# Forty-eight columns of weights, not eight, in the small products of an attention and feed-forward kernel

## The chip, the cores and the metric

The kernel runs on one core of a Trainium2 chip. The metric is the device time of one execution in microseconds (us). Before the change three runs took 989.1, 990.55 and 991.38 us, a median of 990.55 us. Beside these runs one execution was profiled; it took 990.49 us, of which 988.7 us lie between its first and its last instruction (its span).

## The reference

Linear attention with a decaying state, over 4 sequences, 8 heads, 768 steps and 48 elements per head, followed by two feed-forward layers over the 3072 tokens.

```python
for t in range(S):
    cur = np.einsum('bhd,bhe->bhde', u[None] * kt, vt)
    y[:, :, t] = np.einsum('bhd,bhde->bhe', rt, state + cur)
    state = w[None, :, :, None] * state + np.einsum('bhd,bhe->bhde', kt, vt)
x = y as (3072 tokens, 384)
x = (sigmoid(x @ w_gate) * (x @ w_val)) @ w_out      # d_ff 1536
x = (relu(x @ w_in) ** 2) @ w_out2                   # d_ff 2048
```

## The kernel before

**Attention.** The 768 steps are cut into 6 chunks of 128, and a unit is one chunk of one sequence: 24 units. Heads lie in pairs, one on partitions 0 to 47 and one on 64 to 111, and a chunk is two halves of 64 steps. So the attention's products are small: 48 or 64 rows of contraction, 48 or 64 columns of weights, 48 or 64 moving columns, in float32. Each product is two passes, and each pass is a weight load (PEld) and a matrix product (PE) in the trace. Depending on the partitions that a product reads and writes, it runs in one of four quarters of the array (called a tile of the array below): rows 0 to 63 or 64 to 127, output partitions 0 to 63 or 64 to 127. All these products write into one buffer of three PSUM banks, `att`.

For unit n `attn_out` (line 331) issues on TensorE, in this order: 16 products with `am` as moving operand (L270, `att<-am,kv`), 8 that read the state (`reads(0)`, L270), a call of `settle`, the 16 score products of unit n+1 (`attn_scores`, `att<-rT,kT`), a call of `settle` (at the head of `attn_sums`), the 16 sums of unit n+1 (`att<-kv`), a call of `settle`, and 8 more reads (`reads(1)`). After that ScalarE copies the results from PSUM and the sync queue sends them off. `settle` (line 275) is one product of the first 48 partitions of an operand of this unit; its output `tok` is a buffer of the tag `v`, the same one that `pv` of the feed-forward layers uses, and nothing reads it. Over the kernel `settle` is called 72 times: once in `attn_sums(0)`, three times in each of 23 units and twice, without anything between, in the last, which has no unit after it.

**Feed-forward.** Each weight matrix is split into a high and a low float32r part (`convert`: DVE, ScalarE and GpSimd work on each piece), and each product is then three products of 128x128 weights with 512 moving columns (L429 and L448). The order of all instructions is written out by hand: phases 0 to 4 of the first layer run over chunks 0 to 4 with the attention units of the next chunk between their products. `fill(f, j)` calls the attention steps at fixed slots; `attn_out` comes between the gate product (`pg`) and the value product (`pv`). From phase 5 on there are feed-forward products alone.

The first four units run before the first feed-forward phase, with dummy products (`warm`, L590) between them. Units 4 to 7 lie in phase 0, while weights are still loaded and converted; units 8 to 23 in phases 1 to 4.

Of the kernel before, what the change touches and what calls it, by code (L numbers as in the profile page):

```python
# [19 lines left out]
B, H, S, D = 4, 8, 768, 48  # L20
# [22 lines left out]
def tile_kernel(  # L43
# [12 lines left out]
    nc = tc.nc  # L56
# [218 lines left out]
    def settle(x):  # L275

        tok = pp.tile([P, T], F32, tag="v", name="tok")
        nc.tensor.matmul(tok[0:8, 0:8], lhsT=x[0:D, 0:8], rhs=x[0:D, 0:8], start=True, stop=True)  # L278

    def attn_scores(n):  # L280

# [13 lines left out]
    def attn_sums(n):  # L295

        if n >= NU:
            return
        kv = kv_t[n]
        settle(kv)  # L300
        for j in range(HP):
            for q in range(2):
                h = 2 * j + q
                for a in range(2):
                    x = slice(a * L, (a + 1) * L)
                    mm64(
                        1 - a,
                        q,
                        pu[a][64 * q : 64 * q + width[q], j],
                        kv[x, HD + h * D :][:, : width[q]],  # L310
                        kv[x, h * D :][:, :D],
                    )
# [18 lines left out]
    def attn_out(n):  # L331
# [18 lines left out]
        for j in range(HP):  # L350
            for q in range(2):
                h = head(q, j)
                for a in range(2):
                    x = slice(a * L, (a + 1) * L)
                    mm(a, q, j, width[q], kv[x, h * D :][:, : width[q]], am[x, h])
        reads(0)
        settle(kv)
        attn_scores(n + 1)
        attn_sums(n + 1)
        settle(kv)  # L360
        reads(1)
        while len(kv_t) <= n + (4 if len(kv_t) < IN_W + 2 else 3) and len(kv_t) < NU:
# [386 lines left out]
```

## Time and profile before

| what | value |
|---|---|
| median of 3 runs | 990.55 us |
| profiled execution | 990.49 us, span 988.7 us |
| PE busy | 961.3 us (97%), 6904 instructions |
| PEld busy | 764.3 us (77%) |
| DVE, ACT, POOL busy | 453.1, 401.8, 135.0 us |
| mean granted TensorE clock | 0.976 |

PE is TensorE at its products, PEld the same engine at its weight loads, DVE VectorE, ACT ScalarE, POOL GpSimd. The start of a product in the trace is what can be compared; its end is modelled. A product that is the first of a group has its record begin together with its weight load, so its 0.25 to 0.27 us hold the load too, and in a stream one lasts 0.21 or 0.22 us.

### The profile page before, as it was taken

The page shows a single profiled execution, that of the slowest core. Times are in us where ns is not written, and L with a number is a line of the kernel's source. Part 1 is how long each engine was busy: PE and PEld are TensorE (multiplying, and loading weights), DVE is VectorE, ACT ScalarE, POOL GpSimd, SP SyncE. Part 2 cuts the span into 40 slices and gives each one's busy share as a digit, 9 for nine tenths or more (in the row PEclk, how much of TensorE's full clock was granted, in tenths as well). Part 3 has the DMA queues.
Part 4 walks back from the last instruction along what each step waited for, and adds up shares of the span by engine and source line. Part 5 has one row for each costly group of instructions (what it writes and reads, how often), then busy time and mean ns, then how long its engine had stood idle before and what let it go on. Part 6 is the DMA issues. An engine that isn't in the chain of part 4 may idle for free.

```text
span 988.7 us, 16639 instructions
## 1 busy us (share of the span) xinstructions
PE 961.3 (97%) x6904; PEld 764.3 (77%) x6904; DVE 453.1 (46%) x742; ACT 401.8 (41%) x826; POOL 135.0 (14%) x121
## 2 busy tenths in 40 slices
PE   6888899999999999999999999999999999999997
PEld 3566688888888888887888888888888888888886
DVE  5667757754434444422344465343333433433332
ACT  3656756533233223322366564232332322323322
POOL 6446735300000000000033121000000000000000
PEclk7679899999999999999999999999999999999999
DMA  8664555522122221100244440010100100100000
GB/s 302 203 211 126 169 167 161 147 79 84 52 60 89 90 67 27 68 7 15 95 128 123 154 155 1 1 64 1 33 32 1 64 1 1 65 1 1 32 0 33
DMA packets 42235, 76.86 MB, mean 78 GB/s; under 512 B 5168, under 2 KB 17584, under 8 KB 42160
## 3 DMA queue, kind: packets, MB, share of 16 engines
q1 hardware_dynamic: 42160, 75.80, 24.1%
q8 instruction: 54, 0.88, 0.4%
q14 instruction: 21, 0.17, 0.1%
HBM read 60.05 MB, written 11.01 MB: 72 GB/s over the span
## 4 chain that ended last, share of the span: by engine, by line
PE 90%; DVE 4%; ACT 2%; issue 1%; POOL 1%; DMA 1%; SPq 0%; DVEq 0%; ACTq 0%
PE pg L429 34%; PE two L448 16%; PE pv L429 14%; PE po L448 11%; PE att L448 7%; PE att L270 5%; PE pw L590 1%; PE tok L278 1%; DVE first L239 1%; DMA first<-in_rkv 1%; DVE am L319 1%; ACT am L255 1%; POOL wu L134 0%; DVE raw L156 0%; DVE mid L388 0%
## 5 line engine op out<-in xcount | busy, mean ns | idle before, releaser
L429 PE MATMUL pg<-xh,wu 128*128 128x512 f32 x1008 | 315.0, 397 | 5.8 <-ACT wu L133 3.7
L429 PEld LDWEIGHTS pg<-xh,wu 128*128 128x128 f32 x1008 | 189.8, 188 | 54.2 <-ACT wu L133 5.0
L429 PE MATMUL pg<-xl,wu 128*128 128x512 f32 x504 | 195.0, 395 | 0.0
L576 ACT CAST gh<-s 128x512 fp32r<-128x512 f32 (+1 forms) x169 | 104.9, 621 | 194.0 <-DVE s L572 120.6
L412 DVE TENSOR_TENSOR gl<-s,gh 128x512 fp32r<-128x512 f32 x162 | 113.3, 699 | 86.6 <-PE po L448 56.3
L575 DVE TENSOR_TENSOR s<-s 128x512 f32<-128x512 f32 (+1 forms) x97 | 66.6, 687 | 181.4 <-ACT s L574 181.4
L448 PE MATMUL two<-gh,wu 128*128 128x512 f32 x472 | 148.1, 395 | 0.0
L429 PE MATMUL pv<-xh,wu 128*128 128x512 f32 x432 | 141.2, 408 | 0.4 <-POOL wu L134 0.4
L574 ACT ACTIVATE s<-pg 128x512 f32<-128x512 f32 (+1 forms) x97 | 57.6, 594 | 190.3 <-PE pg L429 190.3
L572 DVE TENSOR_TENSOR s<-pv,s 128x512 f32<-128x512 f32 x72 | 49.6, 689 | 176.1 <-PE pv L429 172.6
L429 PEld LDWEIGHTS pg<-xl,wu 128*128 128x128 f32 x504 | 95.0, 189 | 22.7 <-DVE xl L412 0.3
L448 PEld LDWEIGHTS two<-gh,wu 128*128 128x128 f32 x472 | 89.3, 189 | 21.7
L448 PE MATMUL po<-gh,wu 128*128 128x512 f32 (+1 forms) x338 | 105.5, 392 | 0.0
L429 PEld LDWEIGHTS pv<-xh,wu 128*128 128x128 f32 x432 | 81.1, 191 | 21.0 <-POOL wu L134 0.8
L448 PE MATMUL two<-gl,wu 128*128 128x512 f32 x236 | 92.5, 392 | 0.0
L558 ACT ACTIVATE s<-pg 128x512 f32<-128x512 f32 x72 | 43.6, 606 | 110.5 <-PE pg L429 110.2
L429 PE MATMUL pv<-xl,wu 128*128 128x512 f32 x216 | 86.8, 402 | 0.0
L448 PEld LDWEIGHTS po<-gh,wu 128*128 128x128 f32 x338 | 63.4, 188 | 14.6
L154 ACT ACTIVATE raw<-raw 128x384 bf16<-128x384 bf16 x68 | 73.6, 1082 | 0.0
L448 PE MATMUL po<-gl,wu 128*128 128x512 f32 (+1 forms) x169 | 66.2, 392 | 0.0
L448 PE MATMUL att<-gh,wu 128*128 128x512 f32 (+1 forms) x204 | 63.4, 392 | 0.0
L255 ACT ACTIVATE am<-anti,dv 128x64 f32<-128x64 f32 x192 | 50.1, 340 | 16.5 <-DVE dv L245 16.5
(295 smaller groups left out, 919.6 us busy)
## 6 DMA issues: line engine op xcount, KB each, us to landing
raw<-in_w SPq DMA_DIRECT2D x68, 384.0 KB, 3.2
kv<-in_rkv SPq DMA_DIRECT2D x16, 384.0 KB, 3.3
xin<-x2d SPq DMA_DIRECT2D x6, 768.0 KB, 4.2
out<-x2s SPq DMA_DIRECT2D x18, 256.0 KB, 2.0
first<-in_rkv SPq DMA_DIRECT2D x16, 256.0 KB, 5.8
kT<-in_rkv SPq DMA_DIRECT2D x16, 256.0 KB, 4.5
rT<-in_rkv SPq DMA_DIRECT2D x16, 256.0 KB, 5.0
x2d<-x2s SPq DMA_DIRECT2D x15, 256.0 KB, 2.0
```

The costliest lines, as they stand in the source:

```text
L154: nc.scalar.activation(top, top, AF.Prelu, scale=2.0**-112, alpha=2.0**32)
L239: nc.vector.tensor_mul(t, t, two)
L255: nc.scalar.mul(am_t[n][:, h], anti, dv_t[n][:, h : h + 1])
L270: nc.tensor.matmul(out, lhsT=lhsT, rhs=rhs, start=(bank, q) not in opened, stop=True, skip_group_check=True)
L412: (eng or nc.vector).tensor_tensor(out=dst, in0=src, in1=high.bitcast(F32), op=ALU.subtract)
L429: nc.tensor.matmul(ps, lhsT=a, rhs=b_, start=(i == 0), stop=(i == len(pairs) - 1))
L448: nc.tensor.matmul(po[k][:, ts], lhsT=a, rhs=b_[:, ts], start=(first and m == 0), stop=(last and m == 2 and ts is cuts[-1]),)
L558: nc.scalar.activation(s, pg, AF.Sigmoid)
L572: nc.vector.tensor_tensor(out=s[:, ts], in0=pv[:, ts], in1=s[:, ts], op=ALU.mult)
L574: nc.scalar.activation(s[:, ts], pg[:, ts], AF.Relu)
L575: nc.vector.tensor_mul(s[:, ts], s[:, ts], s[:, ts])
L576: nc.scalar.copy(gh[:, ts], s[:, ts])
```

## The change

The product in `settle` takes 48 columns of weights and writes 48 partitions, where it took and wrote 8. Rows, moving columns, buffer and the places of the calls stay.

```diff
     def settle(x):
         tok = pp.tile([P, T], F32, tag="v", name="tok")
-        nc.tensor.matmul(tok[0:8, 0:8], lhsT=x[0:D, 0:8], rhs=x[0:D, 0:8], start=True, stop=True)
+        nc.tensor.matmul(tok[0:D, 0:8], lhsT=x[0:D, 0:D], rhs=x[0:D, 0:8], start=True, stop=True)
```

## Rows read from the trace of the kernel before

**Rows 1.** The page: span, PE's busy time, chain that ended last.
```profile
span 988.7 us, 16639 instructions
...
PE 961.3 (97%) x6904; PEld 764.3 (77%) x6904; DVE 453.1 (46%) x742; ACT 401.8 (41%) x826; POOL 135.0 (14%) x121
...
PE 90%; DVE 4%; ACT 2%; issue 1%; POOL 1%; DMA 1%; SPq 0%; DVEq 0%; ACTq 0%
```

**Rows 2.** Stretches: length, then busy us and count by engine; clock, DMA.
```profile
0.00:127.00 127.00, 104.66 (x1342) 73.66 (x1346) 86.40 (x132) 71.28 (x183) 70.87 (x67) 0.81 0.62 199
127.00:450.00 323.00, 322.94 (x3266) 259.41 (x3266) 156.95 (x278) 124.43 (x305) 29.65 (x22) 1.00 0.27 83
450.00:988.70 538.70, 533.65 (x2316) 431.26 (x2306) 209.70 (x332) 206.09 (x339) 34.50 (x32) 1.00 0.14 46
```

**Rows 3.** Waits of the weight loads, 127 to 450 us: total, times, longest.
```profile
PEld att L270 <- issue: 5.8, 16, 0.4
PEld tok L278 <- PE tok L278: 0.2, 1, 0.2
```

**Rows 4.** Timeline of one unit on TensorE: start, us, engine, line, operation.
```profile
404.46 0.39 PE L429 MATMUL pg<-xl,wu 128*128 128x512 f32 x1
404.78 0.54 PEld L270 LDWEIGHTS att<-am,kv 64*64 64x64 f32 x32 [0.36 <-issue]
404.78 0.68 PE L270 MATMUL att<-am,kv 64*64 64x64 f32 x32
405.22 0.12 PEld L270 LDWEIGHTS att<-rT,state 48*48 48x48 f32 x1
...
405.34 0.21 PE L270 MATMUL att<-rT,state 48*48 48x64 f32 x1
...
405.45 0.21 PE L270 MATMUL att<-rT,state 48*48 48x64 f32 x1
...
405.47 0.21 PE L270 MATMUL att<-rT,mid 48*48 48x64 f32 x1
405.61 0.10 PEld L278 LDWEIGHTS tok<-kv 48*8 48x8 f32 x2
405.62 0.20 PE L278 MATMUL tok<-kv 48*8 48x8 f32 x2
405.74 0.56 PEld L270 LDWEIGHTS att<-rT,kT 48*64 48x64 f32 x32
405.74 0.69 PE L270 MATMUL att<-rT,kT 48*64 48x64 f32 x32
406.37 0.09 PEld L278 LDWEIGHTS tok<-kv 48*8 48x8 f32 x2
406.50 0.54 PEld L270 LDWEIGHTS att<-kv 64*64 64x64 f32 x32
407.09 0.10 PEld L278 LDWEIGHTS tok<-kv 48*8 48x8 f32 x2
407.22 0.12 PEld L270 LDWEIGHTS att<-rT,mid 48*48 48x48 f32 x1
407.45 0.22 PE L270 MATMUL att<-rT,mid 48*48 48x64 f32 x1
407.59 0.19 PEld L429 LDWEIGHTS pv<-xh,wu 128*128 128x128 f32 x1
```

**Rows 5.** Weight loads by line and shape: count, busy us, mean ns, idle before.
```profile
L270 PEld LDWEIGHTS att<-rT,state 48*48 48x48 f32 x256 | 9.4, 119 | 0.0
L270 PEld LDWEIGHTS att<-am,kv 64*64 64x64 f32 x256 | 8.7, 134 | 5.8 <-issue 5.8
L270 PEld LDWEIGHTS att<-am,kv 64*48 64x48 f32 x256 | 8.0, 119 | 0.0
L278 PEld LDWEIGHTS tok<-kv 48*8 48x8 f32 x96 | 4.5, 84 | 3.3 <-PE tok L278 0.2
L278 PEld LDWEIGHTS tok<-first 48*8 48x8 f32 x48 | 2.3, 84 | 3.3 <-ACT th L207 1.4
```

**Rows 6.** Timeline of the last unit's weight loads at its two settles.
```profile
449.33 0.09 PEld L278 LDWEIGHTS tok<-kv 48*8 48x8 f32 x2
449.59 0.09 PEld L278 LDWEIGHTS tok<-kv 48*8 48x8 f32 x2 [0.16 <-PE tok L278]
449.72 0.12 PEld L270 LDWEIGHTS att<-rT,mid 48*48 48x48 f32 x1
```

**Rows 7.** The chain that ended last, start to 130 us: start, us, what.
```profile
20.65 0.13 PE tok L278 x2
...
103.20 0.13 PE tok L278 x2
...
119.56 1.03 POOL wu L134
120.63 2.13 PE pv L429 x8
```

## The prediction

> **What bounds the kernel now.** I read the page first: the span is 988.7 us, PE is busy for 97% of it, and 90% of the chain that ended last is PE [rows 1]. An average hides stages, so the next view is the table of stretches [rows 2]. From 127 to 450 us, where units 8 to 23 lie among feed-forward products, PE is busy for 322.94 of 323.00 us at full clock; from 450 us on there are no settles. Before 127 us PE is busy for 104.66 of 127 us: there other work ends waits too. The view of waits says the same of the middle stretch: the weight loads waited there only for "issue", 16 times, once a unit, and once for a settle [rows 3]. So between 127 and 450 us each nanosecond that TensorE spends on a settle, or stands still beside one, is in the time; before 127 us only part of it.
>
> **What a settle costs now.** The timeline of one unit shows it [rows 4]. The last read ahead of the first settle starts at 405.47; the settle's load starts at 405.61, 0.14 later; the next group's loads start at 405.74, 0.13 after that. From the settle at 406.37 to the next group at 406.50, and from 407.09 to 407.22, it is again 0.13. No wait is printed on these rows, and the 0.13 is far more than two loads of 8 columns need one behind the other: the two together lie in 0.09 or 0.10 us. Elsewhere the loads of a group run ahead without a break: the 48-column load of the reads begins at 405.22, while the last products of the group before, with loads of 64 and of 48 columns [rows 5], are still running (404.78 plus 0.68 is 405.46). So groups of 48 and 64 columns follow each other with no gap, and a gap stands before and behind each product that has 8 columns. The same kind of gap stands where a group of 128 columns follows or precedes: 407.45 to 407.59 (0.14), and 404.46 to 404.78 [rows 4]. What these places have in common is a jump in the shape of the weights, between 8, 48 or 64, and 128. I read the gaps as the array running empty before such a jump.
>
> A page of the Trainium skill bears on this: TensorEngine Tiling (Array Packing), section Tiling Modes, says that a change of the tiling mode, not just of the tile, drains TensorE, and lists modes of 32 and of 64 columns. The gaps agree with it, and by that rule all of them at the settles would go, as in the sum below. No row here names a mode, so the forecast goes by the rows with their 48 columns alone.
>
> **What the change does, step by step.** After it the settle's load has the shape 48*48, that of the reads beside it, and I expect it to run in the stream.
>
> *The longer load.* A load of 48 columns takes 119 ns, one of 8 takes 84 [rows 5]: 35 ns more for each of two passes.
>
> *The stream.* Four tiles of the array work side by side, so 32 passes are 8 rounds. In the reads a round takes 0.055 (405.34 to 405.45 is two). In the scores it is (0.69 - 0.22) / 8 = 0.059: the group's length without the tail of its last product [rows 4]. A settle of 48*48 works in one tile, that of rows 0 to 63 and output partitions 0 to 63, and adds two passes to that tile's work. I price a pass at 0.05: the reads' 0.055, whose 64 moving columns become 8, is the nearest row. The lower bound is nothing, if the other tiles are what each group waits for; the upper is the round of the scores, 0.06.
>
> *One unit.* In the tile that has the settles the work is 8 + 8 + 8 rounds of 0.059 (am, scores, sums; 1.42 us), 4 + 4 rounds of reads at 0.055 (0.44), six passes of settles (0.30) and the gap to the 128-column group behind, which stays (0.14): 2.30 us. Now the unit takes from 404.78 to 407.59, 2.81 us [rows 4]. It gains 0.51, or 0.17 per settle.
>
> *The waits that remain.* Each settle waits for the settle before it, since both write the buffer `v`; with nothing between two of them that costs 0.16, and the second starts 0.26 after the first [rows 6]. In a normal unit a group of 8 rounds (0.47) lies between them, more than 0.26, so nothing new appears. `pv` waits for the third settle; 4 rounds of reads and a gap (0.22 + 0.14) cover it. In the last unit this wait stays: its two settles, now 0.14 + 0.39 from the last read to the next, become about 0.26 and a settle's two passes of 0.06 at most, an estimated gain of 0.15.
>
> *Sum from 127 us on.* Fifteen full units at 0.51 (7.7) and the last one (0.15): 7.8 us. Nothing is late in its place: PE is the bound there with DVE at 156.95 and ACT at 124.43 of 323 us [rows 2].
>
> *Before 127 us.* Here lie 25 settles: the one of unit 0 and three of each of eight units. Twelve of them are on the chain that ended last, the first at 20.65, the last at 103.20 [rows 7]; those off it save nothing. Twelve at 0.17 is 2.0 us, and a little more for those that ran at a lower clock (the stretch has a mean of 0.81 [rows 2]), so 2.5 at most. But each shortens a chain that goes on through ACT, DVE and POOL, and the last wait before PE takes over is for converted weights, POOL at 119.56 [rows 7]. That conversion has its own queue, and where it was nearly as late the gain is lost. Bounds 0 and 2.5; I take 1.4.
>
> Together 9.2 us: 990.49 - 9.2 = **981.3 us**. The profiled execution lies 0.06 under the median, which changes nothing.
>
> If a settle's passes cost nothing, six passes of 0.05 in 15 units (4.5) and the whole early gain (2.5) come in: 7.8 + 4.5 + 2.5 = 14.8, so 975.7. If they cost a full round and nothing early counts: six times 0.01 in 15 units is 0.9 less, 990.49 - 6.9 = 983.6. With a margin the forecast's own range is 975.5 to 984.5.
>
> **The rivals.**
>
> *The gaps stay and the loads are longer: slower.* A settle differs from its neighbours in more than its columns: it writes another buffer, and it occupies one tile alone. If TensorE runs empty at it for one of these reasons, both gaps remain and each settle is 2 times 35 ns longer. That is 47 settles from 127 us on (3.3 us) and the 12 on the early chain (0.8): 4.1 us, **994.6**, from 993.8 to 995.5 if all 72 counted (5.0). For it: no 48*48 product stands alone in this trace. Against it: the am products, reads, scores and sums change partitions and banks among themselves without a gap, and `two` and `po` of the feed-forward layers do too. It decides once less than 0.07 of the roughly 0.24 us per settle goes. The Trainium skill speaks for its price: TensorE: Matmul & The Clock Gate, section LDWEIGHTS, has a load's time proportional to its columns, at 1.2 columns a ns. From that I estimate 33 ns for 40 columns; the measured 35 agrees, and 72 settles would give 4.8 us.
>
> *One of the two gaps stays.* If the array still empties ahead of a settle (0.14 stays) and only the one behind goes, a settle falls from 0.14 + 0.13 + 0.06 for the first round behind to 0.14 + 0.10 + 0.06: 0.03 each, 59 settles, 1.8 us, **988.7**. If the one behind stays and the one ahead goes, 0.10 + 0.10 + 0.06, 0.07 each, 4.1 us, **986.4**. For it: the two gaps are not equally long, so they may not have one cause.
>
> *Nothing changes.* The gaps go, but the passes in the one tile are dearer than priced, as each must wait for the other tiles. At 0.13 a pass the 0.51 of a unit is used up and the time is **990**. Against it: the reads' rounds, where passes of one tile follow each other in 0.055.
>
> **How the numbers follow.** What a measurement of this kernel can tell from no change is 0.2%, 2.0 us. The forecast gets 0.72, one gap of two 0.10 (0.07 of it beyond 0.2%), nothing changes 0.05, longer loads with both gaps 0.13. Faster 0.72 + 0.07 = 0.79; the same 0.03 + 0.05 = 0.08; slower 0.13. A range from 975.5 to 989.0 takes in the forecast and the rival of one gap and leaves out the slower one and no change, 0.18.
>
> **What would show it.** In the trace of the changed kernel the settle's row says 48*48 and its load takes about 119 ns. In the unit near 404 us the load of the settle should start while the reads' products run, not 0.14 after the last, and the next group's first loads should overlap the settle's products; from the first load of `am` to the first of `pv` it should be about 2.30 us. From 450 us on nothing should differ. The forecast is wrong if 0.13 us or more still lies between a settle's load and the next group's, if the unit is 2.8 us or longer, or if PE gains new waits for ACT or DVE between 127 and 450 us.

## The result and the profile after

The changed kernel takes 977.65 us (975.35 to 979.2, four runs), where the kernel before took 990.92 us in the runs beside it (989.1 to 991.38). The ratio is 0.9868 with a 95% interval of 0.9844 to 0.9891: faster by 1.3%. The forecast was 981.3 us, its range 975.5 to 989.0. The profiled execution took 977.92 us with a span of 976.1 us, 12.6 less than before.

The page of the changed kernel, answering [rows 1], shows the same mix: still TensorE, 90% of the chain.

```profile
span 976.1 us, 16639 instructions
...
PE 946.8 (97%) x6904; PEld 757.5 (78%) x6904; DVE 451.3 (46%) x742; ACT 402.3 (41%) x826; POOL 135.6 (14%) x121
...
PE 90%; DVE 4%; ACT 2%; issue 1%; DMA 1%; POOL 1%; SPq 1%; ACTq 0%; DVEq 0%
```

A settle no longer stands apart. The timeline of the unit that answers to [rows 4], on TensorE:

```profile
393.10 0.39 PE L429 MATMUL pg<-xl,wu 128*128 128x512 f32 x1
393.41 0.54 PEld L270 LDWEIGHTS att<-am,kv 64*64 64x64 f32 x32 [0.36 <-issue]
...
394.10 0.18 PEld L278 LDWEIGHTS tok<-kv 48*48 48x48 f32 x2
394.11 0.21 PE L270 MATMUL att<-rT,mid 48*48 48x64 f32 x1
394.16 0.17 PE L278 MATMUL tok<-kv 48*48 48x8 f32 x1
394.16 0.58 PEld L270 LDWEIGHTS att<-rT,kT 48*64 48x64 f32 x32
394.16 0.28 PE L270 MATMUL att<-rT,kT 48*64 48x64 f32 x3
394.18 0.19 PE L278 MATMUL tok<-kv 48*48 48x8 f32 x1
...
394.67 0.18 PEld L278 LDWEIGHTS tok<-kv 48*48 48x48 f32 x2
...
395.24 0.17 PEld L278 LDWEIGHTS tok<-kv 48*48 48x48 f32 x2
...
395.68 0.19 PEld L429 LDWEIGHTS pv<-xh,wu 128*128 128x128 f32 x1
```

The settle's first load starts at 394.10, before the last read's product at 394.11, where it came 0.14 after it. The next group's loads start at 394.16, between the starts of the settle's two products. The unit lasts 395.68 - 393.41 = 2.27 us, where it took 2.81. Settles follow one another by 0.57, eight rounds and two passes.

The loads by shape, answering [rows 5]: 121 ns at full clock where 8 columns took 84, and the idle time before them is nearly gone (3.3 us in each row before).

```profile
L278 PEld LDWEIGHTS tok<-kv 48*48 48x48 f32 x96 | 8.3, 121 | 0.2 <-PE tok L278 0.2
L278 PEld LDWEIGHTS tok<-first 48*48 48x48 f32 x48 | 4.9, 143 | 0.6 <-ACT th L207 0.6
```

The waits of the weight loads in the middle stretch, answering [rows 3], have nothing new (123 to 438 us, with one unit start fewer in it). The wait between the last unit's two settles stays, as in [rows 6].

```profile
PEld att L270 <- issue: 5.5, 15, 0.4
PEld tok L278 <- PE tok L278: 0.2, 1, 0.2
```

The first loads of units 8 and 23 say where the 12.6 us lie. First the kernel before:

```profile
126.87 0.25 PEld L270 LDWEIGHTS att<-am,kv 64*64 64x64 f32 x12 [0.37 <-issue]
448.50 0.20 PEld L270 LDWEIGHTS att<-am,kv 64*64 64x64 f32 x8 [0.36 <-issue]
```

Then the changed one:

```profile
122.79 0.31 PEld L270 LDWEIGHTS att<-am,kv 64*64 64x64 f32 x16 [0.36 <-issue]
436.01 0.20 PEld L270 LDWEIGHTS att<-am,kv 64*64 64x64 f32 x8 [0.36 <-issue]
```

Unit 8 starts 4.1 us earlier. From there to unit 23 it was 321.63 us and is 313.22: 8.4 us for fifteen units, 0.56 from each unit's start to the next. What follows gains 0.1.

### The profile page after: what moved, and what is told of

It is laid out like the page before. It is cut to its first block, busy times and chain, and to the rows that moved or that the text cites. A ratio compares the mean times of both kernels' runs of the same rounds, so it can differ in the third digit from the quotient of the medians.

```text
span 976.1 us, 16639 instructions
## 1 busy us (share of the span) xinstructions
PE 946.8 (97%) x6904; PEld 757.5 (78%) x6904; DVE 451.3 (46%) x742; ACT 402.3 (41%) x826; POOL 135.6 (14%) x121
## 4 chain that ended last, share of the span: by engine, by line
PE 90%; DVE 4%; ACT 2%; issue 1%; DMA 1%; POOL 1%; SPq 1%; ACTq 0%; DVEq 0%
PE pg L429 35%; PE two L448 16%; PE pv L429 15%; PE po L448 12%; PE att L448 7%; PE att L270 5%; DMA first<-in_rkv 1%; DVE first L239 1%; DVE am L319 1%; ACT am L255 1%; POOL wu L134 0%; ACT ys L370 0%; DVE raw L156 0%; PE pw L590 0%; DVE mid L388 0%
```

## The experiments

Each kernel is the kernel before with the settle's product as shown. The runs of before beside them had medians of 989.73 us (32 and 33 columns, the early and the late settles alone), 989.94 (units 2 and 3 alone, every settle twice, the two in other tiles) and 990.82 (128 columns and 32 rows, one run each).

**32 columns and 33 columns: is it the class of the width?**

```diff
-nc.tensor.matmul(tok[0:8, 0:8], lhsT=x[0:D, 0:8], rhs=x[0:D, 0:8], start=True, stop=True)
+nc.tensor.matmul(tok[0:32, 0:8], lhsT=x[0:48, 0:32], rhs=x[0:48, 0:8], start=True, stop=True)
```

> The settle takes 32 columns of weights. Theory (the array empties when the class of width changes, and 32 columns is still another class than 48 and 64): both gaps stay, 0.14 us before and 0.13 us or a little more behind, and the loads are 24 columns longer than with 8 (about 0.02 us each): one unit lasts 2.81 to 2.95 us, total 991 to 994 us. Rival (the gap shrinks gradually with the width of the load): 24 of the 40 columns give 24/40 of the gain of 13.3 us, 983 us, and a unit of about 2.5 us.

Measured: 991.29 us, ratio 1.0015 (1.0004 to 1.0026). Its weight loads in one unit:

```profile
300.65 0.54 PEld L270 LDWEIGHTS att<-am,kv 64*64 64x64 f32 x32 [0.36 <-issue]
301.49 0.13 PEld L278 LDWEIGHTS tok<-kv 48*32 48x32 f32 x2
301.65 0.56 PEld L270 LDWEIGHTS att<-rT,kT 48*64 48x64 f32 x32
...
303.55 0.30 PEld L429 LDWEIGHTS pv<-xh,wu 128*128 128x128 f32 x2
```

With one column more (`tok[0:33, 0:8]`, `lhsT=x[0:48, 0:33]`):

> The settle takes 33 columns of weights, one more than in the run with 32. Theory (class of width): the gaps go as with 48 columns, and each of the six passes is 15 columns shorter, 0.013 us: a unit lasts 2.2 us against 2.27 with 48, total 976 to 978 us. Rival (gradual): 25/40 of the gain, 982.6 us. A second rival (the settle must have just the neighbours' 48 or 64 columns): gaps stay, 991 to 994 us.

Measured: 977.11 us, ratio 0.9869 (0.9854 to 0.9884).

```profile
307.81 0.54 PEld L270 LDWEIGHTS att<-am,kv 64*64 64x64 f32 x32 [0.36 <-issue]
308.50 0.16 PEld L278 LDWEIGHTS tok<-kv 48*33 48x33 f32 x2
308.56 0.57 PEld L270 LDWEIGHTS att<-rT,kT 48*64 48x64 f32 x32
...
310.04 0.30 PEld L429 LDWEIGHTS pv<-xh,wu 128*128 128x128 f32 x2
```

One column separates 2.90 us a unit from 2.23. With 32 the settle begins 0.84 after the unit's first load and the scores 0.16 behind it; with 33 it is 0.69 and 0.06. The gradual rival (983 us for both) is out, and so is the one that the settle must have the neighbours' own width. With both gaps in place the longer load alone makes a unit a little slower: 2.90 us with 32 columns, 2.82 in the kernel before.

**128 columns: upward as well?**

`tok[0:128, 0:8]`, `lhsT=x[0:48, 0:128]`.

> The settle takes 128 columns of weights. Theory (a change of class of width empties the array, upward as well as downward): gaps at every settle as with 8, and longer loads; from the run with 32 columns (24 columns more than 8 gave 0.08 us a unit) 120 columns give 0.4: a unit of about 3.2 us, total about 998 us. Rival (only a narrow load makes the gaps): no gap, six passes of about 0.11 us for 0.05: a unit of about 2.63 us, 984 us.

Measured in one run: 1003.31 us beside 990.82.

```profile
310.30 0.55 PEld L270 LDWEIGHTS att<-am,kv 64*64 64x64 f32 x32 [0.36 <-issue]
311.13 0.29 PEld L278 LDWEIGHTS tok<-kv 48*128 48x128 f32 x2
311.45 0.56 PEld L270 LDWEIGHTS att<-rT,kT 48*64 48x64 f32 x32
...
313.67 0.30 PEld L429 LDWEIGHTS pv<-xh,wu 128*128 128x128 f32 x2
```

The gap ahead of the settle is back: it begins 0.83 after the unit's first load. A unit is 3.37 us, above the 3.2 expected, because the scores' loads begin only behind the settle's two loads of 128 columns (0.32 from settle to scores, 0.29 of it those loads). So it is the jump, not a narrow load, that makes the gap. That the array runs empty in it stays the forecast's reading: a product's end is modelled, and no row shows the array itself.

**32 rows of contraction: columns alone?**

`tok[0:48, 0:8]`, `lhsT=x[0:32, 0:48]`, `rhs=x[0:32, 0:8]`.

> The settle has 48 columns of weights but 32 rows of contraction instead of 48. Theory as the runs show it so far speaks of columns only: then there is no gap and a unit lasts 2.27 us, total 978 us. Extension (the class is that of rows and columns together, and 32 rows are another class than 48 and 64): gaps before and behind each settle, a unit of about 2.95 us, total about 993 us.

Measured in one run: 991.27 us beside 990.82.

```profile
301.33 0.55 PEld L270 LDWEIGHTS att<-am,kv 64*64 64x64 f32 x32 [0.36 <-issue]
302.17 0.16 PEld L278 LDWEIGHTS tok<-kv 32*48 32x48 f32 x2
302.35 0.56 PEld L270 LDWEIGHTS att<-rT,kT 48*64 48x64 f32 x32
...
304.30 0.30 PEld L429 LDWEIGHTS pv<-xh,wu 128*128 128x128 f32 x2
```

A unit is 2.97 us, with both gaps, though the width is 48. So rows count too, which the forecast did not say. The total came out 1.7 us below the 993 expected; one run doesn't resolve that, and the unit's length is read from the trace itself.

**The early and the late settles apart**

```diff
+    calls = [0]
     def settle(x):
...
-        nc.tensor.matmul(tok[0:8, 0:8], lhsT=x[0:D, 0:8], rhs=x[0:D, 0:8], start=True, stop=True)
+        calls[0] += 1
+        m = D if calls[0] <= 25 else 8
+        nc.tensor.matmul(tok[0:m, 0:8], lhsT=x[0:D, 0:m], rhs=x[0:D, 0:8], start=True, stop=True)
```

> 48 columns in the first 25 settles alone (to unit 7), 8 in the other 47. Theory: the gain of the changed kernel is the sum of two independent parts, 0.56 us in each of 15 units from unit 8 on plus 0.25 in the last (8.6 us), and the rest, 4.7 us, in the first eight units, much of it from TensorE's clock rising earlier: total 986 us, with units of 2.81 us later. Rival (the early part of the profile, 4.1 us, was a chance of when the first inputs landed and my 1.4 us is right): 989.5 us.

Measured: 986.09 us, ratio 0.9958 (0.9943 to 0.9972), a gain of 3.6 us. With the condition turned round (8 in the first 25 calls, 48 in the other 47):

> 8 columns in the first 25 settles, 48 in the other 47. Theory: 15 units shorter by 0.56 us and the last by 0.25, 8.6 us in all: 982.3 us, with the work before 127 us as in the kernel before. Rival (early gain by chance): this kernel has nearly the whole gain, 978 to 979 us.

Measured: 981.46 us, ratio 0.9911 (0.9896 to 0.9926), a gain of 8.3 us. The two gains add up to 11.9 us, against 12.6 for 33 columns beside them and 13.3 for the change itself, inside the intervals. Both parts are real, and the early one is far above the 1.4 us of the forecast.

**Units 2 and 3 alone, at half the granted clock**

The condition is `8 <= calls[0] <= 13`.

> 48 columns in the six settles of units 2 and 3 alone, the ones that run at half the granted clock; 8 in all others. Theory (the early gain is larger than forecast because these units shorten by 0.8 us each or more at half clock, and the clock rises sooner behind them): 1.7 to 2.5 us of the 3.6 of the run with the first 25 settles, total 987.3 to 988 us. Rival (early gain comes evenly from all settles, 3.6/25 each): 0.9 us, 988.9 us.

Measured: 987.85 us, ratio 0.998 (0.9971 to 0.999), a gain of 2.0 us (1.0 to 2.9 by the interval): about half of the early gain from six of 25 settles, with the rival's 0.9 just outside. How the clock answers is seen in three stretches: length, then busy us and count of PE, PEld, DVE, ACT, POOL, then the granted clock. The kernel before:

```profile
30.00:35.00 5.00, 4.70 (x119) 4.08 (x120) 2.51 (x6) 1.67 (x7) 2.17 (x3) 0.50 0.93 293
35.00:41.50 6.50, 5.48 (x121) 3.99 (x120) 2.99 (x6) 2.98 (x12) 0.77 (x1) 0.50 0.75 243
41.50:49.40 7.90, 7.77 (x26) 2.85 (x25) 6.12 (x11) 7.14 (x19) 4.23 (x4) 0.69 0.54 152
```

The changed kernel:

```profile
30.00:35.00 5.00, 3.97 (x99) 2.92 (x98) 2.88 (x5) 3.16 (x13) 2.94 (x3) 0.50 1.02 323
35.00:41.50 6.50, 6.50 (x103) 4.07 (x97) 4.29 (x11) 3.70 (x14) 0.24 (x1) 0.62 0.66 211
41.50:49.40 7.90, 7.15 (x116) 4.05 (x116) 5.48 (x6) 4.32 (x7) 4.72 (x4) 1.00 0.74 222
```

And 48 columns in units 2 and 3 alone:

```profile
35.00:41.50 6.50, 6.01 (x136) 3.88 (x138) 6.08 (x13) 5.32 (x20) 1.57 (x3) 1.00 0.88 288
```

Unit 3 begins with the first row of each pair below and ends with the second, the first dummy product's load. Before it takes 4.54 us:

```profile
36.91 0.93 PEld L270 LDWEIGHTS att<-am,first 64*64 64x64 f32 x32 [1.93 <-DVE am L319]
41.45 0.13 PEld L590 LDWEIGHTS <-idle 128*128 128x128 bf16 x2
```

In the changed kernel 3.72:

```profile
33.91 0.93 PEld L270 LDWEIGHTS att<-am,first 64*64 64x64 f32 x32 [1.94 <-DVE am L319]
37.63 0.13 PEld L590 LDWEIGHTS <-idle 128*128 128x128 bf16 x2
```

In the third kernel, already at the clock's upper level (2.4 GHz), it takes 2.09 (35.33 to 37.42). So unit 3 gains 0.8 us at half clock, where 0.51 had been priced. The lower clock is not the main reason for that. Unit 1, from its first load to the first dummy product's, ran at full clock in both kernels and gained 0.71. The kernel before:

```profile
24.56:27.36 2.80, 2.80 (x118) 2.42 (x118) 2.77 (x5) 2.05 (x6) 2.72 (x3) 1.00 0.23 55
```

The changed kernel:

```profile
23.52:25.61 2.09, 2.09 (x118) 2.01 (x118) 2.06 (x5) 2.07 (x6) 1.35 (x1) 1.00 0.34 103
```

Units 0 to 3 are the first chunk of each sequence and skip the reads of the state, half of their reads (in `reads`, `if a or c`). The tile with the settles then has 4 rounds of reads instead of 8, and the forecast's own sum with 0.22 in place of 0.44 is 2.08 us.

The stretch behind unit 3 runs at 0.62 and 1.00 of full clock instead of 0.50 and 0.69. Over the first 127 us the clock does not tell the kernels apart: the changed kernel and the one with 32 columns, which keeps its gaps, have the same mean of 0.85, where the kernel before has 0.81 [rows 2]. From 28 to 50 us it does, in one profiled execution of each. With the gaps in units 2 and 3 the mean is 0.61 to 0.69 (before, 32 columns, 128 columns, 32 rows, late settles alone); without them it is 0.77 (changed, 33 columns, early settles alone, every settle twice) or 0.92 (units 2 and 3 alone, the two in other tiles). What a higher clock there is worth in the total was not measured by itself.

**The price of a pass: every settle twice**

```diff
+for _ in range(2):
+    nc.tensor.matmul(tok[0:D, 0:8], lhsT=x[0:D, 0:D], rhs=x[0:D, 0:8], start=True, stop=True)
```

> Each settle issues its 48-column product twice, into the same place. Theory (a settle without gaps costs just its passes, in the one tile that does the most work): six passes more per unit at 0.045 to 0.05 us, a unit of 2.54 to 2.57 us, and with the early units 982 to 984 us. Rival (the other tiles cover them): unit 2.27 us, 977.5 us. Second rival (each settle still costs a wait of its own): above 2.6 us a unit, 985 us or more.

Measured: 984.1 us, ratio 0.9934 (0.992 to 0.9949). The first load of the unit and the first of `pv`:

```profile
310.33 0.54 PEld L270 LDWEIGHTS att<-am,kv 64*64 64x64 f32 x32 [0.36 <-issue]
...
312.87 0.30 PEld L430 LDWEIGHTS pv<-xh,wu 128*128 128x128 f32 x2
```

2.54 us, 0.27 more than 2.27 for six more passes: 0.045 each. They lie on the path. Both rivals are out: the other tiles do not cover the passes, and no wait of its own shows beside them.

**Another tile of the array, and two**

With 33 columns, written to `tok[64:97, 0:8]`, so in the tile of output partitions 64 to 127:

> The settle has 33 columns of weights and writes partitions 64 to 96, so that its passes lie in another tile of the array, whose sums have 48 columns of weights and not 64 and so take less time. Theory (the tile with most work sets a unit's length): 8 rounds of sums there are about 0.11 us shorter, a unit of 2.10 to 2.14 us against 2.23 with 33 columns in the first tile, total 975 to 976 us. Rival (all tiles wait for a settle): 2.23 us and 977 us.

Measured: 973.32 us, ratio 0.9836 (0.9819 to 0.9852).

```profile
304.37 0.55 PEld L270 LDWEIGHTS att<-am,kv 64*64 64x64 f32 x32 [0.36 <-issue]
...
306.47 0.30 PEld L429 LDWEIGHTS pv<-xh,wu 128*128 128x128 f32 x2
```

```diff
+calls[0] += 1
+o = 64 * (calls[0] % 2)
+nc.tensor.matmul(tok[64:97, 0:8], lhsT=x[o : o + D, 0:33], rhs=x[o : o + D, 0:8], start=True, stop=True)
```

> As the run in the other tile with 33 columns, but every second settle reads partitions 64 to 111 and so lies in a third tile, whose sums are as short. Theory (tile with most work): four or two passes per unit in each of the two, a unit of 2.02 to 2.08 us, total 973 to 975 us. Rival (a settle in another row half has to wait for the settle before it): units of 2.2 us or longer, 977 us or more.

Measured: 972.1 us, ratio 0.9818 (0.9803 to 0.9832).

```profile
303.36 0.55 PEld L270 LDWEIGHTS att<-am,kv 64*64 64x64 f32 x32 [0.36 <-issue]
...
305.39 0.19 PEld L433 LDWEIGHTS pv<-xh,wu 128*128 128x128 f32 x1
```

2.10 and 2.03 us a unit: the tile with most work sets its length, as the forecast's sum had it. Both totals came out under what was expected, by 1.7 and 0.9 us, though the units are as expected: unit 8 starts at 120.22 and 119.95 us in these traces and at 122.63 with 33 columns in the first tile, so that part lies before it. The version with two tiles is the fastest found, 0.5 to 0.6% under the changed kernel by the medians, and on its units by 0.24 us; its interval overlaps that of the run with one other tile.

A kernel without the settles was not tried. Nor was it tested what order of the writes to PSUM the settles keep, and what keeps it once the gaps are gone.

## Why the prediction was right, and where its size was off

**The gaps, right.** They go, both of them, because 48 columns are no jump from their neighbours. The forecast called the 0.13 behind a settle far more than its two loads need; by [rows 4] these loads take 0.09 or 0.10 of it, so only 0.03 or 0.04 lies beyond them. What went is the 0.14 ahead and most of the loads' own time, which now overlaps with other loads. The trace and the pair of 32 and 33 columns show it; the rivals "both gaps stay", "one stays" and "nothing changes" are out. The Trainium skill, TensorEngine Tiling (Array Packing), section Tiling Modes, lists modes by rows and by columns of 32, 64 and 128 and a drain at a change of mode: the runs with 32, 33 and 128 columns and with 32 rows agree on each count. The forecast read the jump off the columns alone; the run with 32 rows adds the rows.

**One unit, right.** Forecast 2.30 us, measured 2.27; gain forecast 0.51, measured 0.54 in the unit shown and 0.56 from one unit's start to the next. The pass was priced at 0.05 and is 0.045, shown by doubling it. That the passes lie in one tile which sets the unit's length is shown by moving them.

**From 127 us on, right and a little low.** Forecast 7.8 us, measured 8.4 and 0.1 in the trace, 8.3 in the run with the late settles alone. Nothing became late in its place: PE shows no new wait there. The last unit's gain was put at 0.15 and is 0.10, since its second settle still waits for the first.

**Before 127 us, mis-sized.** The term was 1.4 us with bounds of 0 and 2.5. It measures 4.1 in the trace and 3.6 in the run with the early settles alone, above the upper bound. Two steps of it failed. The first is the price: 0.17 per settle, a third of what a unit with all its reads gains, was taken for the units before 127 us too. Units 0 and 1 went from 2.80 us to 2.14 and 2.09, 0.66 and 0.71 less at nearly full or full clock, and unit 3 gained 0.83 at half clock. The second is the path: settles off the chain that ended last were to save nothing. Unit 2's three are not named on that chain, but it had a piece of "issue" while unit 2 ran, and this piece shrank by 1.51 us, as unit 2 did (4.55 to 3.04, its beginning at a higher clock than before). The chain of the kernel before, then of the changed one:

```profile
31.68 3.33 issue
```

```profile
30.18 1.82 issue
```

With these four units, unit 4 begins 3.83 us earlier (51.77 and 47.94). A part of the 4.1 is chance: unit 8 begins at 126.87, 126.39, 125.17 and 125.14 us in the profiled executions of four kernels with early gaps and 8 to 48 columns (before, late settles alone, 32 rows, 32 columns), and at 122.79, 123.03 and 122.63 in three without (changed, early settles alone, 33 columns). That is 2.1 to 4.2 us, and the profile of before is the latest of the four. That the whole was a chance of when the inputs landed was a rival, and the two half-changes exclude it.

Of the 3.4 us between the forecast and the profiled execution (981.3 and 977.92) 2.7 are this term and 0.7 the middle stretch. The range held partly by luck: its lower end allowed 4.5 us for passes that cost nothing, and they cost 0.045 each; that room took in the early gain, which was over its own bound.

**The longer load, right.** 84 ns became 121, but it lies in the stream. Where the gaps stay it shows: with 32 columns a unit is 0.08 us longer than with 8.

## What to carry to other kernels

Before shrinking a small matrix product, look at its neighbours. Among products with 48 or 64 rows and 48 or 64 columns of weights, one with 8, 32 or 128 columns or with 32 rows got a gap ahead of it, and one with 33 or 48 columns and 48 rows did not. A settle with 8 columns took 0.27 us out of the stream (0.14 ahead of it and 0.13 to the next group), three times its two passes of 0.045 without the gaps. A group's length is the work of the tile of the array that has most of it, so products that can go anywhere belong in another tile. A stage whose units differ (here half the reads, half the clock) has to be priced from its own rows, and what a shorter stage does to the clock behind it is a term of its own.

## What the runs showed of the hardware that was not expected

Products in different tiles do not keep the program's order. In the sums of [rows 4] the program ends with four passes of 48 columns, behind four of 64. In the kernel before, the 48-column products follow one another by 0.045 us in each tile, those of 64 by 0.058, and the last of 48 columns start at 406.86 and 406.87, ahead of the last of 64 at 406.94 and 406.95. From 407.08 to 407.09, by the modelled ends, only products with 64 columns still run:

```profile
L270 PE MATMUL att<-kv 64*64 64x48 f32 x4 | 0.3, 218 | 0.0
```

The Trainium skill, TensorE: Matmul & The Clock Gate, section Part 3: Packing small matmuls — row/col tiling, says that products start and end strictly in the program's order. For products in different tiles this trace does not agree. Whether a product passes a settle is not shown: the scores' first three, at 394.16, stand ahead of the settle's second at 394.18, but their records begin with their loads.

A jump costs the same 0.14 us ahead of a settle for 8 columns as for 32 and 128: the settle began 0.83, 0.84 and 0.83 us after the unit's first load. Behind it the next group's loads begin 0.02 to 0.04 us after the settle's own have ended, with 8, 32 and 128 columns and with 32 rows (0.13 less 0.10 or 0.09, 0.16 less 0.13, 0.32 less 0.29, 0.18 less 0.16). With 33 columns they begin 0.10 before that end (0.06 against 0.16).
